# Ten more filler products on TensorE, and a new hand-written order for the opening of an attention and feed-forward kernel

## The chip, the cores and the metric

The kernel runs on one core of one Trainium2 chip. What counts is the device time of one execution in microseconds (us), as the median of several runs. Its engines are TensorE (PE in the profile, with its weight loads as PEld), VectorE (DVE), ScalarE (ACT), GpSimd (POOL) and SyncE (SP), whose queue issues the DMA transfers.

## What is computed

Attention over keys and values that are first averaged in groups of 8, then a gated feed-forward layer on its output, with weights given in 64-bit floating point. Cut to what matters:

```python
# q, k, v: (8 batches, 8 heads, 576, 64), float32; w_in (512, 2048), w_out (2048, 512), float64
k_p = k.reshape(B, H, Sp, 8, D).mean(axis=3)          # Sp = 72
v_p = v.reshape(B, H, Sp, 8, D).mean(axis=3)
scores = (q @ k_p^T) / sqrt(D)
attn = softmax(scores)                                # with max subtracted, sum + 1e-9
x = (attn @ v_p) as 4608 rows of 512
h = x @ w_in
out = (h * clip(h + 3, 0, 6) / 6) @ w_out
```

## The kernel before

The 4608 rows of x are worked in ten blocks (512, 256, 384, six of 512, 384). For each block TensorE makes h for one of 16 slices of d_ff (`Step.h`, L782: twelve products, three for each quarter c of d_model, since x and the weights are split into a high and a low part), ScalarE and VectorE gate it, and `Step.out` (L813) adds its products into the output. In the gaps of a block's steps the attention of the next block is made.

The first block has nothing ahead of it, so there is an opening: k and v of batch 0 are loaded and averaged, the scores of the first four tiles of 128 queries are made (half A, two tiles; half B, two tiles; two groups g of four heads each), the attention is transposed, multiplied with v, split into xhi and xlo, and meanwhile the first weights are turned from 64-bit words into float32 and split.

The steps of the opening that the texts name:

- `busy(n)` (L270): n products of the identity with itself into a PSUM tile `idle` that nobody reads. 13 stand first, 3 later.
- `prep_k` (L214 on VectorE, L222 on ScalarE): averages k. The first four (VectorE's 0 to 3) are batch 0; VectorE's 87, 93, 99 and 100 are the four of batch 1, which the opening doesn't need; 87 waits for the transfer kst that is SP's number 14.
- `Scores`: `product` (L412, TensorE), `top` (L416, VectorE, negative maximum), `exps` (L420, ScalarE), or for one tile of half A, called x11, `shift` (L427, VectorE), `exp` (L430, ScalarE) and `total` (L433, VectorE); then `invert` (L436, L437) and `divide` (L448, L454, on VectorE or GpSimd). x00, x10, x01, x11 are half A (the second digit is g); b[0] to b[3] are half B.
- `FirstValues.heads` (L290): sixteen products that average v; `transposes_of_half` (L507, L509), whose results VectorE or ScalarE copies (L510, L511). VectorE's number 54 is the copy for half B, g = 1: the last thing that the last two `av` of the block wait for.
- `av` (L583): attention times v, two products each; VectorE's `xlo` (L589) splits what comes out.
- `Prep` of weights: `scale` (L695) and `low` (L684) on ScalarE, `sign` (L689) and `join` (L700) on VectorE, `hi` (L723, ScalarE), `lo` (L728, VectorE). The h of slice f needs the `lo` of f.
- `pool_second` (L385, VectorE): averages v of batch 1.

Up to the fourth step of the first block the order of the instructions on every engine is not that of the program text. `put_in_order` takes the instructions of that window, numbers them for each engine in program order, and chains them in the order of the table `ORDER`. SP's entries are the order in which the loads are issued. An engine works strictly in its order, so an instruction that waits holds all that stand behind it.

Of the kernel before, what the change touches and what calls it, by code (L numbers as in the profile page):

```python
# [30 lines left out]

ORDER = {
    "PE": """
        0-12 17-18 13-16 19-45 50-53 56-57 46-49 54-55 60-63 58-59 64-68 78-79 69-71 80-85 88-89 72-74 86-87
        75-77 100-101 96-99 102-108 118-126 109-111 211-214 112-117 93-95 90-92 127-144 230-233 145-147 246-247
        148-156 166-171 157-159 163-165 266-267 160-162 193-195 184-189 172-180 190-192 196-198 181-183 218-223
        199-201 208-210 277-278 297-298 202-204 299 215-217 205-207 224-229 251-253 240-242 234-236 248-250
        243-245 237-239 254-259 279-281 260-262 268-270 263-265 274-276 315-316 282-287 306-308 288-296 334-336
        303-305 271-273 300-302 309-314 323-328 317-322 337-342 349-350 362-364 331-333 343-345 329-330 346-348
        354-356 365-367 357-359 368-376 385-387 360-361 380-381 351-353 382-384 388-390 377-379 391-393 419-421  # L40
        394-396 400-402 409-411 397-398 406-408 403-405 422-427 451-453 438-440 428-430 399 441-443 454-456
        431-433 416-418 457-462 444-446 412-415 479-481 466-468 434-437 476-478 469-472 447-450 463-465 482-493
        473-475 536-537 503-505 494-496 530-532 562-563 544-546 497-499 547-549 533-535 538-540 582-583 541-543
        500-502 512-514 509-511 550-555 515-517 506-508 556-558 518-523 576-578 559-561 564-569 579-581 524-526
        584-589 570-572 527-529 573-575
    """,
    "DVE": """
        3 2 1 0 4-8 87 11 15 9 12 17 16 10 18 13 19 14 20-21 23 22 24 26 34 28 40 64 29 25 61 32 30 33 62 36 35
        37 27 39 38 47 31 43-44 41 65 55 93 45 50 49 51 63 52-53 56 54 42 48 59-60 57-58 99 74 46 100 77 73 106
        76 75 79 81 78 82 111 80 107 121 86 108 83-84 112 67 110 85 113 90 88 109 89 68 94 114 91-92 115 131 96  # L50
        98 95 101 136 97 103 66 143 105 102 116 104 137 118 117 132 122 120 126 119 128 133 127 130 129 144 140
        123 138 147 139 142 141 72 149 145 70-71 146 124 69 152 125 135 148 151 150 154 156 134 159 153 157 155
        166 158 160-161 168 170 167 163 172 162 169 173 164-165 171 174-175 178-179 187 183 181 184-186 188 194
        176 189 182 177 190 199 191 180 200 192 201 193 195 197-198 202 196 203
    """,
    "Activation": """
        3 2 0-1 4-18 27 19 34 21 20 25 23 82 22 24 81 28-32 35-38 46 26 33 53 40-43 54 44 47-50 52 56 51 60 55
        39 59 69 89 61 57-58 45 88 74 96 95 71 67 70 75 68 97 104-107 98 72 76 79 73 80 77 108-111 86 78 83-84
        93 62 90 85 87 94 117-120 91 126-129 99 102 92 115 103 100 112 136 65 130 137 101 138-139 116 113 124
        121 114 125 122 140 123 143 66 63 131 64 132 134 144 135 153 133 145 141 147 142 150 148 146 154 151 149  # L60
        155 157 160 156 152 166 158 161 159 167 170-172 162-163 168 164 173 165 174 176 178 169 175 183 177
        180-181 179 187 186 184 188 185 194-197 189 202-205 198-199 182 200 208-211 190-191 201 206 192 207
        212-213 193
    """,
    "Pool": """
        0-1 12 2-3 18 4 7-8 10 5 9 6 14 13 16 15 17 11 19-20 24 21 23 22
    """,
    "SP": """
        2-3 1 0 4-5 8 6-7 14 9 11 10 22-24 21 20 13 12 15 18 16 19 25-26 28 31 17 27 32 34 33 29 41 30 44 51 35
        48 46 43 36 47 39 52 59 42 37-38 45 40 50 49 53-55 57-58 60 56  # L70
    """,
}

# [2 lines left out]
def attention_moe_kernel(  # L76
# [190 lines left out]
    def busy(n):  # L267

        for _ in range(n):
            nc.tensor.matmul(idle, ident, ident, start=True, stop=True)  # L270
# [609 lines left out]
    for s in x:  # L880
        s.product()
    values.rest()
    busy(3)
    values.heads(0)
    values.heads(1)
    for s in x:
# [211 lines left out]
```

## Time and profile before

| | |
|---|---|
| median of 3 runs | 924.62 us (923.67, 924.62, 924.62) |
| the profiled execution's own time | 923.03 us |
| span of the profiled execution, first to last instruction | 921.2 us |
| TensorE busy | 908.1 us (99%) |
| VectorE, ScalarE busy | 457.4 us (50%), 461.7 us (50%) |
| granted clock of TensorE, mean | 0.998 |

The profiled execution has 1.8 us outside of its span (923.03 less 921.2). The median of the three runs lies 1.6 us above it. Busy time of TensorE is modelled from starts and pipelined ends, so it says that TensorE has something in flight and not that it is at its peak.

### The profile page before, as it was taken

To read this page: it belongs to the slowest core of one execution; us is meant where nothing else is said; L and a number is where in the kernel's file an instruction comes from. 1 tells how busy PE (TensorE), PEld (TensorE's weight loads), DVE (VectorE), ACT (ScalarE), POOL (GpSimd) and SP (SyncE) were. 2 spreads that over 40 slices of the span, in tenths; PEclk is the share of its full clock that TensorE was granted. 3 is DMA by queue.
4 is the path that set the end of the run, shared out by engine and by line. 5 is a ranking of instruction groups with operands and counts; after the bars stand their busy time and mean duration, and the time that the engine had idled before them with its cause. 6 is when DMAs were issued, how large, how long until landed. Compare 5 with 4: busy or idle time off the path is not lost.

```text
span 921.2 us, 12671 instructions
## 1 busy us (share of the span) xinstructions
PE 908.1 (99%) x4548; PEld 776.8 (84%) x4548; DVE 457.4 (50%) x916; ACT 461.7 (50%) x1340; POOL 82.0 (9%) x167
## 2 busy tenths in 40 slices
PE   7899999999999999999999999999999999999998
PEld 7688889999888888888888888888888888888997
DVE  6999855475356333824356326633356234332322
ACT  6898665465355434633456335633545344333322
POOL 4100001021000100101011101110101001100000
PEclk9999999999999999999999999999999999999999
DMA  9960203050031002300042004100210010000100
GB/s 313 393 242 1 92 12 121 1 166 19 0 115 58 24 1 80 104 12 6 1 145 57 12 1 134 61 12 1 92 42 23 1 41 18 0 1 3 45 1 35
DMA packets 41935, 57.19 MB, mean 62 GB/s; under 512 B 7568, under 2 KB 23696, under 8 KB 41872
## 3 DMA queue, kind: packets, MB, share of 16 engines
q1 hardware_dynamic: 41728, 56.37, 19.0%
q8 instruction: 36, 0.59, 0.3%
q14 instruction: 27, 0.22, 0.1%
q10 hardware_dynamic: 144, 0.00, 0.0%
HBM read 46.93 MB, written 9.44 MB: 61 GB/s over the span
## 4 chain that ended last, share of the span: by engine, by line
PE 96%; DVE 2%; DMA 1%; SPq 0%; ACT 0%; issue 0%; DVEq 0%
PE pso L813 43%; PE psh L782 43%; PE psa L583 4%; PE psa L412 4%; PE psa L518 2%; DMA kst<-k_l 1%; PE psa L520 0%; DVE u L689 0%; ACT stage L420 0%; DVE u L700 0%; SPq L257 0%; DVE stage L448 0%; SPq L259 0%; DVE a L510 0%; SPq L262 0%
## 5 line engine op out<-in xcount | busy, mean ns | idle before, releaser
L782 PE MATMUL psh<-xhi,w 128*128 128x512 f32 (+2 forms) x1288 | 402.3, 372 | 0.0
L813 PE MATMUL pso<-w,ghi 128*128 128x512 f32 (+1 forms) x1184 | 367.0, 391 | 0.0
L782 PEld LDWEIGHTS psh<-xhi,w 128*128 128x128 f32 x1288 | 238.0, 188 | 36.1 <-issue 0.4
L813 PEld LDWEIGHTS pso<-w,ghi 128*128 128x128 f32 x1184 | 214.1, 188 | 36.0
L782 PE MATMUL psh<-xlo,w 128*128 128x512 f32 (+2 forms) x644 | 237.5, 369 | 0.0
L794 DVE SCALAR_TENSOR_TENSOR g<-g,psh 128x512 f32<-128x512 f32 (+2 forms) x161 | 101.4, 630 | 271.6 <-ACT g L790 270.4
L813 PE MATMUL pso<-w,glo 128*128 128x512 f32 (+1 forms) x592 | 225.9, 386 | 0.0
L790 ACT ACTIVATE g<-psh,small 128x512 f32<-128x512 f32 (+2 forms) x161 | 103.7, 644 | 209.7 <-PE psh L782 193.3
L782 PEld LDWEIGHTS psh<-xlo,w 128*128 128x128 f32 x644 | 121.3, 188 | 18.2
L802 DVE TENSOR_TENSOR glo<-g,ghi 128x512 fp32r<-128x512 f32 (+2 forms) x161 | 102.7, 638 | 62.1 <-ACT ghi L798 60.2
L813 PEld LDWEIGHTS pso<-w,glo 128*128 128x128 f32 x592 | 111.1, 188 | 21.7
L798 ACT CAST ghi<-g 128x512 fp32r<-128x512 f32 (+2 forms) x161 | 92.9, 577 | 70.6 <-DVE g L794 67.9
L420 ACT ACTIVATE e<-psa,mx 128x72 f32<-128x72 f32 x256 | 78.5, 322 | 50.8 <-DVE mx L416 50.1
L448 POOL TENSOR_TENSOR a<-e,sm 128x256 f32<-128x256 f32 x60 | 41.2, 687 | 517.2 <-PE pso L813 180.3
L420 ACT ACTIVATION_READ_ACCUMULATOR e<-psa,mx 128x1 f32 x256 | 52.8, 206 | 0.0
L416 DVE TENSOR_REDUCE mx<-psa 128x4 f32<-128x288 f32 x72 | 32.3, 454 | 29.2 <-PE psa L412 28.8
L412 PEld LDWEIGHTS psa<-kbd,qt 128*128 128x128 f32 x288 | 43.1, 189 | 4.2
L412 PE MATMUL psa<-kbd,qt 128*128 128x144 f32 x288 | 45.5, 285 | 0.0
L585 ACT COPY x<-psa 128x192 f32<-128x192 f32 (+7 forms) x60 | 23.0, 387 | 32.6 <-PE psa L583 32.4
L332 DVE TENSOR_REDUCE vsum<-vst 128x64 f32<-128x512 f32 (+1 forms) x36 | 37.8, 1068 | 2.3 <-DMA vst<-v_l 1.5
L436 DVE TENSOR_SCALAR sm<-sm 128x4 f32<-128x4 f32 x72 | 12.4, 176 | 48.7 <-ACT e L420 45.7
L529 ACT CAST ahi<-psa 128x256 fp32r<-128x256 f32 (+1 forms) x70 | 24.6, 353 | 18.8 <-PE psa L518 9.8
(93 smaller groups left out, 628.9 us busy)
## 6 DMA issues: line engine op xcount, KB each, us to landing
out<-o SPq DMA_DIRECT2D x35, 256.0 KB, 2.3
raw<-w_in_l SPq DMA_DIRECT2D x16, 512.0 KB, 8.4
raw<-w_out_l SPq DMA_DIRECT2D x16, 512.0 KB, 9.1
kst<-k_l SPq DMA_DIRECT2D x28, 288.0 KB, 3.2
qt<-q_l SPq DMA_DIRECT2D x28, 256.0 KB, 3.2
vst<-v_l SPq DMA_DIRECT2D x24, 256.0 KB, 3.0
vst<-vr_l SPq DMA_DIRECT2D x36, 64.0 KB, 1.9
stage<-k_l SPq DMA_DIRECT2D x4, 288.0 KB, 3.6
```

The costliest lines, as they stand in the source:

```text
L332: nc.vector.tensor_reduce(out=vs[:n, p], in_=st[:n, : POOL * D].rearrange("p (o d) -> p d o", o=POOL), axis=AX.X, op=ALU.add)
L412: nc.tensor.matmul(to, qt[:, p, :], kbds[b % 2][:, p, :], start=r == 0, stop=r == last)
L416: nc.vector.tensor_reduce(out=self.mx, in_=self.ps, axis=AX.X, op=ALU.max, negate=True)
L420: nc.scalar.activation(self.e[:, h], self.ps[:, h], AF.Exp, bias=self.mx[:, h : h + 1], accum_out=self.sm[:, h : h + 1])
L448: engine.tensor_tensor(out=self.a[:, : 4 * D].rearrange("p (h s) -> p h s", h=4), in0=e[:, :, :D], in1=sm[:, :, None].broadcast_to([P, 4, D]),
L583: nc.tensor.matmul(ps, l, r, start=n == 0, stop=n == len(mms) - 1)
L782: nc.tensor.matmul(self.ps, l[f][:, c, :], r[:, c, :], start=c == 0 and i == 0, stop=c == NCC - 1 and i == 2)
L790: nc.scalar.activation(self.g, self.ps, AF.Relu, bias=half, scale=1.0 / (6.0 * WSCALE))
L794: nc.vector.scalar_tensor_tensor(out=g, in0=g, scalar=1.0, in1=self.ps, op0=ALU.min, op1=ALU.mult)
L798: nc.scalar.copy(self.ghi, self.g)
L802: nc.vector.tensor_tensor(out=self.glo, in0=self.g, in1=self.ghi.bitcast(F32), op=ALU.subtract)
L813: nc.tensor.matmul(pos, l, r[:, cols], start=f == 0 and i == 0, stop=f == NF - 1 and i == 2)
```

## The change

`busy(3)` between the scores' products and `values.heads` becomes `busy(13)`: ten more products that nobody reads. In program order they are TensorE's numbers 24 to 33, so that every later number of TensorE's list is 10 higher than before (`heads` was 24 to 39 and is 34 to 49). And `ORDER`, the whole table, is another one. The first lines of each engine, before and after; the other lines of the lists of TensorE, VectorE and ScalarE are replaced too:

```diff
 "PE"
-0-12 17-18 13-16 19-45 50-53 56-57 46-49 54-55 60-63 58-59 64-68 78-79 69-71 80-85 88-89 72-74 86-87
-75-77 100-101 96-99 102-108 118-126 109-111 211-214 112-117 93-95 90-92 127-144 230-233 145-147 246-247
+0-12 21 13-14 22 15-18 23 19-20 24 34-49 62-63 25 50-55 26 66-67 64-65 68-69 27-28 56-59 74-75 60-61
+70-71 88-89 72-73 29-30 76-81 31 90-93 32 82-87 33 94-95 98-99 96-97 106-121 128-130 122-124 131-136
 "DVE"
-3 2 1 0 4-8 87 11 15 9 12 17 16 10 18 13 19 14 20-21 23 22 24 26 34 28 40 64 29 25 61 32 30 33 62 36 35
-37 27 39 38 47 31 43-44 41 65 55 93 45 50 49 51 63 52-53 56 54 42 48 59-60 57-58 99 74 46 100 77 73 106
+0 3 1-2 4-6 87 7-9 11 15 12 10 13 17 14 18 26 23 22 24 19 16 32 20 33 28-29 93 21 25 64 55 65 27 35 34
+43 40 36 30 37 31 38-39 61 99 50 41 44 51 47 45 52-53 62 49 56 54 48 100 42 59 57 46 60 58 74 63 73
 "Activation"
-3 2 0-1 4-18 27 19 34 21 20 25 23 82 22 24 81 28-32 35-38 46 26 33 53 40-43 54 44 47-50 52 56 51 60 55
+0-15 17 16 19 18 82 20 28-31 21 25 81 53 24 54 26 22-23 27 34-38 32 88 33 40-43 89 47-50 39 46 44 56 52
 "Pool"
-0-1 12 2-3 18 4 7-8 10 5 9 6 14 13 16 15 17 11 19-20 24 21 23 22
+0-1 12 2-3 18 7 4 8 11 5-6 13 9-10 17 14-16 19-22 24 23
 "SP"
-2-3 1 0 4-5 8 6-7 14 9 11 10 22-24 21 20 13 12 15 18 16 19 25-26 28 31 17 27 32 34 33 29 41 30 44 51 35
+3 0-2 4-5 8 7 14 6 9-10 13 12 15 23-24 22 11 16 20-21 19 17-18 25-26 28-29 32 34 30-31 33 27 48 41 44 51
@@ between the scores of half A and values.heads(0) @@
-    busy(3)
+    busy(13)
```

In words, for what the texts speak of. On TensorE: of the thirteen fillers that now stand at the second `busy`, four lie between the products of half A's scores, one after them, and the rest singly or in pairs between the later groups; the last is ahead of 84 and 85 (before's numbers; 94 and 95 after), the transposes of half B's last 32 columns, g = 0. The product of b[0] goes ahead of half A's transposes. What stands ahead of the last two `av` of the block is the same work as before, besides fillers. On VectorE: 87 goes ahead of `top` and `shift` of x11 (7 and 8); 99 goes ahead of 54, and 63 (a `pool_second` piece) behind it. On ScalarE: 17, the `scale` of the first weights, goes ahead of 16, the `exp` of x11. On SP: kst (14) goes ahead of vr (6), the second half of q (10) ahead of the second part of the first weights (11).

## Rows read from the trace of the kernel before

**Rows 1.** The page, busy time of each engine over the span.
```profile
PE 908.1 (99%) x4548; PEld 776.8 (84%) x4548; DVE 457.4 (50%) x916; ACT 461.7 (50%) x1340; POOL 82.0 (9%) x167
```

**Rows 2.** The chain that ended last: start us, us, what.
```profile
5.59 7.24 DMA kst<-k_l
...
33.41 0.61 DVE a L510
...
34.07 3.50 PE psa L583 x8
```

**Rows 3.** Windows: stretch, length, PE, PEld, DVE, ACT, POOL busy (instructions), clock, DMA share, GB/s.
```profile
10.00:15.00 5.00, 3.35 (x30) 3.16 (x29) 3.15 (x15) 4.31 (x24) 3.18 (x5) 1.00 1.04 380
...
200.00:921.00 721.00, 717.50 (x3501) 610.19 (x3499) 310.71 (x634) 318.75 (x949) 57.36 (x114) 1.00 0.13 38
```

**Rows 4.** The same columns, microsecond by microsecond around 34 us.
```profile
34.00:35.00 1.00, 0.93 (x3) 0.82 (x4) 1.00 (x4) 1.00 (x2) 0.00 (x0) 0.69 1.07 342
35.00:36.00 1.00, 1.00 (x4) 0.82 (x3) 1.00 (x2) 0.96 (x3) 0.00 (x0) 0.50 1.03 393
36.00:37.00 1.00, 1.00 (x4) 0.74 (x3) 1.00 (x2) 0.56 (x2) 0.00 (x0) 0.50 1.04 414
37.00:38.00 1.00, 1.00 (x6) 0.91 (x5) 0.28 (x1) 0.39 (x2) 0.00 (x0) 0.60 1.03 410
```

**Rows 5.** Windows, PE alone: stretch, length, busy (instructions), clock, DMA share, GB/s.
```profile
10.40:34.07 23.67, 16.65 (x110) 1.00 1.05 373
```

**Rows 6.** Windows, DVE alone, same columns: ahead of and behind the copy of half B.
```profile
12.85:34.01 21.16, 20.71 (x53) 1.00 1.05 372
...
34.01:49.64 15.63, 14.32 (x21) 0.89 1.04 397
```

**Rows 7.** Timeline of PE: start us, us, instruction, count, idle before it and releaser.
```profile
9.65 0.83 PE L270 MATMUL idle<-ident 128*128 128x128 f32 x6
12.13 3.84 PE L290 MATMUL psa<-stage,ident 128*128 128x128 f32 x32 [1.65 <-DMA stage<-v_l]
...
17.61 1.22 PE L412 MATMUL psa<-kbd,stage 128*128 128x144 f32 x8 [0.77 <-DMA stage<-q_l]
...
32.48 0.60 PE L507 MATMUL psa<-ident,stage 128*128 128x128 f32 x4
34.07 0.94 PE L583 MATMUL psa<-a,v 128*128 128x256 f32 x2 [0.98 <-DVE a L510]
...
50.13 0.63 PE L782 MATMUL psh<-xhi,w 128*128 128x512 f32 x2
```

**Rows 8.** Timeline of DVE, same columns.
```profile
8.87 1.68 DVE L416 TENSOR_REDUCE mx<-psa 128x4 f32<-128x288 f32 x4 [1.54 <-PE psa L412]
10.58 0.46 DVE L427 TENSOR_TENSOR stage<-psa,mx 128x288 f32<-128x288 f32 x1
12.85 0.75 DVE L214 TENSOR_REDUCE ksum<-kst 128x72 f32<-128x576 f32 x1 [1.81 <-DMA kst<-k_l]
14.36 0.41 DVE L448 TENSOR_TENSOR stage<-stage,sm 128x256 f32<-128x256 f32 x1
...
30.96 0.39 DVE L385 TENSOR_TENSOR v<-v 128x256 f32<-128x256 f32 x1
...
33.33 0.68 DVE L510 COPY a<-psa 128x512 f32<-128x512 f32 x1
...
48.42 1.23 DVE L728 TENSOR_TENSOR w<-u,w 128x1024 fp32r<-128x1024 f32 x1
```

**Rows 9.** Timeline of ACT, same columns.
```profile
12.94 0.51 ACT L430 ACTIVATE stage<-stage 128x288 f32<-128x288 f32 x1
14.13 0.68 ACT L695 ACTIVATE raw<-raw 128x512 f32<-128x512 f32 x1 [0.69 <-DMA raw<-w_in_l]
```

**Rows 10.** Windows, all engines: what the DMA engines moved (last column, GB/s).
```profile
4.00:12.80 8.80, 7.15 (x49) 6.96 (x48) 5.02 (x9) 4.72 (x27) 1.71 (x2) 1.00 1.05 335
...
14.10:17.60 3.50, 2.74 (x25) 2.51 (x24) 3.50 (x11) 3.35 (x7) 3.38 (x6) 1.00 1.08 304
```

More of the change, by code (lines that the diff above doesn't have):

```diff
@@ L33 @@
     "PE": """
-        0-12 17-18 13-16 19-45 50-53 56-57 46-49 54-55 60-63 58-59 64-68 78-79 69-71 80-85 88-89 72-74 86-87
-        75-77 100-101 96-99 102-108 118-126 109-111 211-214 112-117 93-95 90-92 127-144 230-233 145-147 246-247
-        148-156 166-171 157-159 163-165 266-267 160-162 193-195 184-189 172-180 190-192 196-198 181-183 218-223
-        199-201 208-210 277-278 297-298 202-204 299 215-217 205-207 224-229 251-253 240-242 234-236 248-250
-        243-245 237-239 254-259 279-281 260-262 268-270 263-265 274-276 315-316 282-287 306-308 288-296 334-336
@@ L39 @@
[L39 to L43, printed above, removed]
@@ L44 @@
-        500-502 512-514 509-511 550-555 515-517 506-508 556-558 518-523 576-578 559-561 564-569 579-581 524-526
-        584-589 570-572 527-529 573-575
+        0-12 21 13-14 22 15-18 23 19-20 24 34-49 62-63 25 50-55 26 66-67 64-65 68-69 27-28 56-59 74-75 60-61
+        70-71 88-89 72-73 29-30 76-81 31 90-93 32 82-87 33 94-95 98-99 96-97 106-121 128-130 122-124 131-136
+        125-127 100-102 137-139 221-224 240-243 103-105 140-148 152-154 149-151 155-157 256-257 158-160 179-181
+        176-178 161-163 173-175 170-172 164-169 182-184 203-205 200-202 185-193 197-199 194-196 225-227 231-233
@@ new lines @@
+        206-211 218-220 212-217 276-277 234-239 261-263 228-230 258-260 244-249 253-255 264-272 250-252 281-283
+        278-280 287-291 273-275 292-294 307-309 284-286 295-297 313-315 310-312 304-306 298-303 319-321 316-318
+        325-326 344-346 322-324 333-335 327-332 336-338 359-360 341-343 364-366 372-374 347-352 361-363 375-377
+        353-355 378-380 390-391 381-386 339-340 356-358 367-369 395-400 370-371 392-394 387-389 401-406 410-412
+        429-431 407-408 413-415 432-437 409 438-440 416-418 448-450 441-443 419-421 426-428 444-447 451-453
@@ L46 @@
+        422-425 476-478 454-460 464-466 479-482 467-472 546-547 473-475 461-463 492-494 483-485 495-497 572-573
+        498-503 489-491 486-488 510-512 504-509 592-593 540-542 516-518 543-545 522-524 554-556 548-553 557-562
+        513-515 566-568 563-565 519-521 525-527 569-571 574-576 528-530 586-588 577-579 589-591 594-596 531-533
+        597-599 534-539 583-585 580-582
     """,
     "DVE": """
-        3 2 1 0 4-8 87 11 15 9 12 17 16 10 18 13 19 14 20-21 23 22 24 26 34 28 40 64 29 25 61 32 30 33 62 36 35
@@ L49 @@
-        37 27 39 38 47 31 43-44 41 65 55 93 45 50 49 51 63 52-53 56 54 42 48 59-60 57-58 99 74 46 100 77 73 106
[L50 to L53, printed above, removed]
@@ L54 @@
-        176 189 182 177 190 199 191 180 200 192 201 193 195 197-198 202 196 203
+        0 3 1-2 4-6 87 7-9 11 15 12 10 13 17 14 18 26 23 22 24 19 16 32 20 33 28-29 93 21 25 64 55 65 27 35 34
+        43 40 36 30 37 31 38-39 61 99 50 41 44 51 47 45 52-53 62 49 56 54 48 100 42 59 57 46 60 58 74 63 73
+        76-77 79 106 75 81 78 82 80 111 84 83 66 86 88 85 121 68 90 89 67 112 92 91 94 96 95 98 101 97 103 113
+        107 102 108 105 110 109 116 131 104 118 115 117 114 120 126 136 128 119 143 138 122 130 127 71 70 72 69
@@ L55 @@
+        137 129 123 140 142 139 149 144 125 141 147 145 132 152 148 151 124 154 146 156 133 150 159 134 157 153
+        155 166 158 161 160 135 168 163 167 164-165 162 169 172-173 170 175 171 187 174 178 194 179 176 195 188
+        196 189 186 183 177 181 184-185 182 180 199 190 200 191-193 197-198 201-203
     """,
     "Activation": """
-        3 2 0-1 4-18 27 19 34 21 20 25 23 82 22 24 81 28-32 35-38 46 26 33 53 40-43 54 44 47-50 52 56 51 60 55
-        39 59 69 89 61 57-58 45 88 74 96 95 71 67 70 75 68 97 104-107 98 72 76 79 73 80 77 108-111 86 78 83-84
@@ L59 @@
[L59 to L63, printed above, removed]
+        0-15 17 16 19 18 82 20 28-31 21 25 81 53 24 54 26 22-23 27 34-38 32 88 33 40-43 89 47-50 39 46 44 56 52
@@ new lines @@
+        60 96 51 55 95 59 45 57 69 98 58 70 97 67 71 68 62 74-76 72 104-107 73 79 77 61 80 83 78 108-111 66 86
+        84 87 65 85 90 93 91 94 99 102 92 103 100 115 112 101 116 113 63 117-120 64 121 114 126-129 124 131 136
+        125 122 137-138 134 130 123 135 153 132 144 139 143 140 133 147 150 141 145 142 148 146 160 155 154 162
+        157 149 151 166 161 152 156 158-159 163 167 171 164-165 168 170 172 169 175 173 178-179 174 180 183
+        194-197 181 176-177 189 202-205 188 187 186 184 182 185 198 208-211 199-201 206 190 207 191 212 192 213
@@ L64 @@
+        193
     """,
     "Pool": """
-        0-1 12 2-3 18 4 7-8 10 5 9 6 14 13 16 15 17 11 19-20 24 21 23 22
+        0-1 12 2-3 18 7 4 8 11 5-6 13 9-10 17 14-16 19-22 24 23
     """,
     "SP": """
-        2-3 1 0 4-5 8 6-7 14 9 11 10 22-24 21 20 13 12 15 18 16 19 25-26 28 31 17 27 32 34 33 29 41 30 44 51 35
-        48 46 43 36 47 39 52 59 42 37-38 45 40 50 49 53-55 57-58 60 56
+        3 0-2 4-5 8 7 14 6 9-10 13 12 15 23-24 22 11 16 20-21 19 17-18 25-26 28-29 32 34 30-31 33 27 48 41 44 51
@@ L71 @@
+        47 43 35 52 36 40 39 37-38 45-46 42 50 49 59 53-54 56 58 55 57 60
     """,
```

## The prediction

> **What bounds the kernel now.** I read the page first: TensorE is busy for 99% of the span [rows 1], so the end moves only with time in which TensorE has nothing to do or runs slowly. The windows say where that is: hardly any after 200 us, some in the opening [rows 3]. Between 10.40 and 34.07 us TensorE is busy for 16.65 of 23.67 us, so it waits for 7.02 us [rows 5]; from 34.07 on it never stops. The chain of waits confirms it: before 34.07 us the chain runs over a transfer and over VectorE, and at 34.07 it passes to TensorE, from VectorE's copy for half B (number 54), and stays there [rows 2]. The moment at which that copy ends, 34.01 us, decides when the unbroken stretch begins [rows 7, 8].
>
> The second loss is the clock. In the windows around 34 us the granted clock falls to half (1.2 of 2.4 GHz) just after TensorE takes up its work, and is full again before 38 us [rows 4]. What TensorE did before: it ended its transposes at about 33.1 us and stood until 34.07, after a stretch of short pieces of work [rows 5, 7]. The missing shares are 0.31 + 0.50 + 0.50 + 0.40 of a microsecond, together 1.71 us of full-speed work, and TensorE had work for all of it [rows 4].
>
> What sets the copy's time? VectorE's windows: from 12.85 us, when kst lands and 87 starts, to 34.01 us it is busy for 20.71 of 21.16 us [rows 6]. Ahead of that it stood for 1.81 us, waiting for kst, with nothing behind it that it could have done sooner than its order allows [rows 8]. So the opening before is bound by VectorE, from the landing of kst to 54.
>
> **The fillers.** Three fillers show six records; the last five starts are (0.83 - 0.27) us apart in total, 0.11 us each, with some 0.27 us for the last one alone, so a filler takes 0.22 us [rows 7]. Ten take 2.2 us. They are free if they fall into waits, of which there are 7.02 us [rows 5]; the last one stands ahead of two transposes of half B, after which TensorE still waits for VectorE twice. I take nothing; without that cover they cost up to 2.2 us.
>
> **VectorE's order.** Up to and with 54 its list is the same set of instructions, except that 99 comes in (as long as 87, 0.75 us) and 63 goes out (0.39 us) [rows 8]. More important is 87: it now stands ahead of x11's `top` (one of four in 1.68 us: 0.42) and `shift` (0.46). Before, these two ran while VectorE would have waited for kst anyhow; now they wait behind 87 and are done after the landing [rows 8]. From 87 to the end of 54 VectorE therefore has 20.71 + 0.42 + 0.46 + 0.75 - 0.39 = 21.95 us of work.
>
> It starts when kst lands. SP issues it one place earlier, ahead of vr with its 128 KB; at the 335 GB/s of that stretch this is 0.38 us [rows 10], so 12.47 us. Without any wait 54 ends at 34.42 us.
>
> Two waits come in. First, x11's `exp` on ScalarE stands behind `scale` of the first weights, which starts when these land, at 14.13 us, and takes 0.6 net; `exp` takes 0.5, so it ends at about 15.2 [rows 9]. VectorE reaches `total` after 87, 7, 8, five small ones at some 0.08 and a divide of 0.41: 12.47 + 0.75 + 0.42 + 0.46 + 0.40 + 0.41 = 14.9. Wait: 0.3 to 0.4, I take 0.35. Second, `top` of b[0] needs b[0]'s product, which before waited until 17.61 us for the second half of q [rows 7]. q now goes right behind the first weights: 14.13 us plus 512 KB at 304 GB/s, 1.7 us [rows 10], is 15.8, and I take 16.0, since its pieces are small. Product and latency add 0.7: 16.7. VectorE is there at 15.2 + 0.35 (`total`) + 0.5 (divide) + 0.05 = 16.1. Wait: 0.6. Were q as late as before, 17.61, it would be 2.2. So 54 ends at 34.42 + 0.35 + 0.60 = 35.4, between 34.4 (no wait) and 37.0 (0.35 and 2.2). GpSimd's vr lands later too, by the 288 KB of kst (0.9 us), but half A's transposes then find b[0]'s product ahead of them, which hides it; other waits behind ScalarE I count as nothing, since I step through about even with VectorE there.
>
> TensorE so takes up the last two `av` at 35.45 instead of 34.07: a loss of 1.4 us (0.4 to 3.0).
>
> **The clock.** With fillers between the groups the clock should stay full, and 1.71 us come back. No filler stands in the last wait, which is now longer: all work ahead of the copy is done by about 33.1 us as before, so TensorE stands for 2.3 us where it stood for 0.98 [rows 7]. Below, this is the rival.
>
> **Does the stream stay unbroken?** Before, VectorE had `lo` of slice 3 ready at 48.42 + 1.23 = 49.65 us and TensorE used it first at 50.13 + 0.23: some 0.7 us ahead [rows 7, 8]. After the change VectorE's work from 54 to there is 14.32 - 0.75 + 0.39 = 13.96 us [rows 6, 8], ending at 49.4 without waits. TensorE's need, with the full clock, comes (50.36 - 34.07) - 1.71 = 14.6 us after 35.45, at 50.0. So it holds, with 0.6 us to spare; VectorE waited 1.31 us in that stretch before [rows 6], and if it does so again TensorE loses up to 0.7. I take nothing, and keep 0.7 for the range.
>
> Sum: +1.4 - 1.7 = -0.3 us. The profiled execution's span goes from 921.2 to 920.9, its time from 923.03 to 922.7; the median of 924.62, which lies 1.6 above it, to 924.3.
>
> **The rivals.**
>
> 1. *The clock falls all the same.* The fillers stand early, and the wait ahead of the copy grows from 0.98 to 2.3 us. For it: half speed came before after a shorter wait. Against: the work before that wait is denser (fillers, and groups gathered). It is decided by whether half speed is granted between 33 and 37 us. Price: the -1.71 is gone, +1.4, and with VectorE's waits +0.7: 926.0 to 926.7, slower. This is also the case that the change doesn't do what it says.
>
> 2. *The timed runs of before never had the fall.* One profile shows it, and I can't see the others; their median is even longer. Then nothing comes back, and +1.4 stays: 926.0. What speaks against it is only the one trace in hand [rows 4]. The Trainium skill bears on this: "TensorE: Matmul & The Clock Gate", Part 1, says that the switching isn't tied to the kernel's start, so that its moment differs between runs of one kernel; no row here shows that, since there is one trace.
>
> 3. *VectorE doesn't lose its place.* If kst landed by 10.2 us, when `top` of x10 is done [rows 8], 87 would cost no wait, and 54 would end 2.3 us earlier than I say, at 33.1; with the clock full: 924.62 - 0.9 - 1.7 = 922.0, faster. Against it: kst landed at 12.83 [rows 2], and one place in the queue is 0.38 us.
>
> **Chances.** Forecast 0.60; its own range is -1.3 (54 at 34.4, full clock) to +2.0 (54 at 37.0 and 0.7 for `lo`), so 923.3 to 926.6. Rival 1 0.18, rival 2 0.14, rival 3 0.08. The bound of 0.2%, about what a measurement can tell, is 1.85 us. Faster than that is rival 3 and a little more: 0.10. Slower than that is half of rival 1, a third of rival 2 (each with the later VectorE) and the top of the forecast's range: 0.22. Same: 0.68. For 8 in 10 I take 922.6 to 926.9: at the low end the forecast's end and 0.7 for rival 3, at the high end rival 1 with its waits.
>
> **What would show it.** Right: VectorE's first batch-1 reduction at about 12.5 us with two instructions of x11 behind it; the copy for half B ending near 35.4; no half clock; an unbroken TensorE from there; ScalarE's `scale` ahead of `exp` at 14.1. Wrong: half clock in 33 to 38 us (rival 1); other profiles of before without it (rival 2); the copy before 34 us (rival 3); waits of TensorE for `lo` after 40 us; q landing near 17.6.

## The result, and the profile after

The changed kernel takes 927.68 us (median of 6 runs, 926.51 to 928.86), against 923.35 us for the kernel before, timed beside it (6 runs, 921.42 to 924.62): a ratio of 1.0048, 95% interval 1.0031 to 1.0064. It is slower by 4.3 us, beyond the range of 922.6 to 926.9. The profiled execution of it took 928.31 us with a span of 926.2 us, 5.0 us more than the span before. One later run of the kernel before took 1521.48 us at a mean granted clock of 0.557 and is left out of every figure.

One thing that stands ahead of the prediction has to be put right. The table's window ends at the fourth step of the *second* block (`j == 1 and u == 3`), at about 143 us, so the table orders the whole first block too. And what the table does not name is put in order when the program is recorded, starting from where the table ends: a comparison of the two traces, engine by engine, shows other orders up to about 225 us, and the same order from there on.

The opening first. Windows of the kernel after answer to [rows 3 to 6]; the columns are stretch, length, busy of PE, PEld, DVE, ACT, POOL (instructions), clock, DMA share, GB/s:

```profile
10.40:36.89 26.49, 20.08 (x134) 16.57 (x132) 23.33 (x56) 21.99 (x84) 8.97 (x16) 1.00 1.05 360
12.93:36.84 23.91, 18.16 (x118) 14.84 (x116) 23.00 (x55) 19.41 (x67) 8.97 (x16) 1.00 1.05 365
36.84:49.64 12.80, 12.75 (x69) 11.17 (x70) 12.72 (x19) 11.69 (x25) 0.00 (x0) 1.00 1.05 387
```

No half clock, as forecast. VectorE is still the engine that sets the end of the opening: busy for 23.00 of 23.91 us from the landing of kst to the copy for half B. But that stretch was to be 22.9 us long (21.95 of work and 0.95 of waits), and kst was to land at 12.47. VectorE's timeline after answers to [rows 8]:

```profile
12.93 0.75 DVE L215 TENSOR_REDUCE ksum<-kst 128x72 f32<-128x576 f32 x1 [2.25 <-DMA kst<-k_l]
13.60 0.45 DVE L417 TENSOR_REDUCE mx<-psa 128x4 f32<-128x288 f32 x1
14.08 0.46 DVE L428 TENSOR_TENSOR stage<-psa,mx 128x288 f32<-128x288 f32 x1
14.45 0.78 DVE L437 TENSOR_SCALAR sm<-sm 128x4 f32<-128x4 f32 x3
...
15.41 1.07 DVE L449 TENSOR_TENSOR stage<-stage,sm 128x256 f32<-128x256 f32 x1
...
17.32 0.44 DVE L417 TENSOR_REDUCE mx<-psa 128x4 f32<-128x288 f32 x1
...
24.00 0.69 DVE L386 TENSOR_TENSOR stage<-stage 96x512 f32<-96x512 f32 x1 [0.88 <-DMA stage<-vr_l]
...
36.16 0.68 DVE L511 COPY a<-psa 128x512 f32<-128x512 f32 x1
```

The order is the one described: 87, then x11's `top` and `shift`, both now behind the landing. The copy ends at 36.84 us, where 35.4 was forecast. The two waits for `exp` and for b[0]'s product did not come (no bracket at 14 to 18 us). Instead three small instructions at 14.45 took 0.78 us and a divide at 15.41 took 1.07, where the same divide took 0.41 [rows 8], and a transfer of vr is waited for at 24.00. GpSimd's timeline shows what ran beside them: its two large additions of vr, which in the kernel before ran from 11.01 to 13.06 us, since vr was then issued ahead of kst.

```profile
13.80 2.06 POOL L302 TENSOR_TENSOR stage<-stage 32x512 f32<-32x512 f32 x2 [10.05 <-DMA stage<-vr_l]
```

ScalarE and TensorE, against [rows 7, 9]. ScalarE's `scale` is ahead of `exp`, b[0]'s product starts at 16.41 us (17.61 before), and TensorE takes up the last two `av` at 36.89 instead of 34.07:

```profile
14.80 0.69 ACT L696 ACTIVATE raw<-raw 128x512 f32<-128x512 f32 x1 [1.54 <-DMA raw<-w_in_l]
15.38 0.44 ACT L431 ACTIVATE stage<-stage 128x288 f32<-128x288 f32 x1
```
```profile
16.41 0.73 PE L413 MATMUL psa<-kbd,stage 128*128 128x144 f32 x4 [0.85 <-DMA stage<-q_l]
...
35.71 0.38 PE L510 MATMUL psa<-ident,stage 128*96 128x128 f32 x2
36.89 0.70 PE L584 MATMUL psa<-a,v 128*128 128x256 f32 x2 [0.79 <-DVE a L511]
```

Now what the prediction did not look for. Two windows of the stretch that was to stay unbroken, before and then after (columns as above):

```profile
140.00:150.00 10.00, 10.00 (x67) 9.10 (x67) 4.46 (x12) 4.55 (x16) 2.71 (x6) 1.00 0.61 178
200.00:210.00 10.00, 10.00 (x56) 9.17 (x55) 8.79 (x20) 7.85 (x28) 1.50 (x3) 1.00 0.33 94
```
```profile
140.00:150.00 10.00, 9.23 (x55) 7.83 (x54) 3.44 (x10) 5.72 (x18) 2.09 (x5) 1.00 0.57 174
200.00:210.00 10.00, 8.74 (x45) 7.14 (x44) 8.65 (x18) 7.27 (x29) 1.47 (x4) 1.00 0.52 136
```

TensorE was busy throughout both before, and stands in both after. At 140 us the timelines of TensorE, of its weight loads and of ScalarE say why:

```profile
140.01 0.39 PE L814 MATMUL pso<-w,glo 128*128 128x512 f32 x1
141.17 0.73 PE L814 MATMUL pso<-w,ghi 128*128 128x512 f32 x2 [0.77 <-ACT o L820]
```
```profile
141.17 0.30 PEld L814 LDWEIGHTS pso<-w,ghi 128*128 128x128 f32 x2 [1.19 <-ACT o L820]
```
```profile
140.21 0.40 ACT L799 CAST ghi<-g 128x256 fp32r<-128x256 f32 x1 [1.96 <-PE pso L814]
140.52 0.59 ACT L820 ACTIVATE o<-pso 128x512 f32<-128x512 f32 x1
```

TensorE can go on when ScalarE has emptied a PSUM bank (`o`). That copy stands in ScalarE's order behind a `ghi` which itself waits, for 1.96 us, for TensorE. The weight loads stand for 1.19 us there; this is the wait that the experiments look for.

At 200 us VectorE holds the stream up. VectorE after:

```profile
196.60 0.52 DVE L795 SCALAR_TENSOR_TENSOR g<-g,psh 128x384 f32<-128x384 f32 x1
198.56 2.05 DVE L333 TENSOR_REDUCE vsum<-vst 128x64 f32<-128x512 f32 x2 [1.43 <-DMA vst<-v_l]
200.53 0.55 DVE L803 TENSOR_TENSOR glo<-g,ghi 128x384 fp32r<-128x384 f32 x1
...
203.86 0.55 DVE L795 SCALAR_TENSOR_TENSOR g<-g,psh 128x384 f32<-128x384 f32 x1
```

The averaging of the next v waits for its transfer and stands ahead of `glo`, which TensorE needs. Before, `glo` stood ahead of the same pair, which waited for 0.31 us:

```profile
195.06 0.55 DVE L802 TENSOR_TENSOR glo<-g,ghi 128x384 fp32r<-128x384 f32 x1
...
196.01 2.05 DVE L332 TENSOR_REDUCE vsum<-vst 128x64 f32<-128x512 f32 x2 [0.31 <-DMA vst<-v_l]
```

TensorE after waits several times between 201 and 204.5 us, the last two of them:

```profile
203.37 0.76 PE L413 MATMUL psa<-kbd,qt 128*128 128x144 f32 x4 [0.93 <-ACT e L421]
204.47 0.45 PE L783 MATMUL psh<-xhi,w 128*128 128x384 f32 x1 [0.34 <-DVE g L795]
```

How far the profiled execution of after lies behind that of before can be counted by the work that TensorE has done (the products of each trace added up at their usual lengths, fillers left out). The lag is 2.8 us at 34 us and 1.2 at 38 us, because the execution before has lost 1.7 us to its half clock in between. It is 1.0 at 100 us, 2.4 from 143 us, and 4.55 from 230 us to the last product; the rest of the 5.0 lies behind that. So the stretch around 140 us costs 1.3 us and the one around 200 us 2.2.

### The profile page after: what moved, and what is told of

It reads as the page before. It is cut to its first block, busy times and chain, and to the rows that moved or that the text cites. A ratio compares the mean times of both kernels' runs of the same rounds, so it can differ in the third digit from the quotient of the medians.

```text
span 926.2 us, 12708 instructions
## 1 busy us (share of the span) xinstructions
PE 911.2 (98%) x4568; PEld 778.1 (84%) x4568; DVE 457.5 (49%) x916; ACT 461.0 (50%) x1340; POOL 79.2 (9%) x167
## 4 chain that ended last, share of the span: by engine, by line
PE 94%; DMA 3%; DVE 1%; SPq 1%; ACT 0%; issue 0%; DVEq 0%
PE pso L814 42%; PE psh L783 42%; PE psa L584 4%; PE psa L413 4%; PE psa L519 1%; DMA raw<-w_out_l 1%; DMA raw<-w_in_l 1%; DMA vst<-v_l 1%; PE psa L521 0%; DVE vsum L333 0%; DVE v L386 0%; SPq L258 0%; DVE a L511 0%; SPq L260 0%; ACT stage L421 0%
```

## The experiments

Every kernel here fixes the order of all instructions, to the end of the program, so that the rest can't be put in another order by an edit of the opening:

```diff
+        window[1:] = [len(traced)]      # the table now names every instruction
```

"Old" and "new" are the orders before and after. The kernel before was timed again beside them, four times: medians 922.76 (27 runs), 923.06 (27), 922.93 (32) and 923.29 (17). Numbers 1 to 4 belong to the first, 5 to 8 to the second, 9 to 12 to the third, 13 and 14 to the fourth. "Full clock" below means a mean granted clock of 0.999 or 1.0: in the profiles of numbers 2 and 14, which have 0.999, the clock is full as long as TensorE works from 5 us on and falls only in the last 2 us, behind its last product.

**1. Old order everywhere, fixed.** What the fixing itself does, and whether the half clock is always there.

> The kernel before, with the order of every engine written out to the end, the same order that it had: its time is that of before. Its runs list the granted clock of each execution. Theory (the half clock is a matter of chance): some executions have a mean clock of 0.998 and some 1.0, and those with the full clock are up to 1.7 us shorter. Rival (the half clock belongs to this order): every execution has 0.998.

922.95 us, ratio 1.0011 (1.0001 to 1.0022): near nothing. The runs of the kernel before beside it have a mean granted clock of 1.0 in 11 of 27; these average 922.05 us, the 12 with 0.998 average 923.38. Over all four timings 41 of 103 runs have 1.0 and 61 have 0.998 or less, and the difference between 1.0 and 0.998 is 1.3 to 2.2 us. So a half clock like that of [rows 4] is an event of some executions, and rival 2 was right for four in ten. A run lists the mean alone, not the place. The profiles show that the place differs as well: the clock is half from about 34 to 40.6 us in number 1's, and from about 13.3 to 16.7 us in number 9's, whose 922.37 us is the fastest of its eleven runs.

**2 and 3. New opening with the old rest, and old opening with the new rest.** The table's part (to about 143 us) from one order, what stands behind it from the other.

```diff
 # 2: new_opening_old_rest                     # 3: old_opening_new_rest
-"PE" <old table>  <old rest>                  -"PE" <old table>  <old rest>
+"PE" <new table, with fillers>  <old rest>    +"PE" <old table>  <new rest>
```

> The changed kernel's opening (table and fillers), and behind it, to the end of the program, the order that the kernel before had. Theory (the rest of the program was put in another order, and that costs some 3.5 us at 141 us and at 201 to 204 us): span about 922.3, 1 us above before, and no wait of TensorE at these two places. Rival (the opening hands on its lateness, and the waits come whatever the order of the rest): span 925 to 926, as the changed kernel.

> The opening of the kernel before with three fillers, and behind it the order that the rest of the changed kernel had. Theory (the order of the rest costs some 3.5 us): span about 924.7, with TensorE's waits near 140 us and 200 us. Rival (the lateness of the opening makes them): span 921 to 922.

Measured: 925.82 (1.0031, 1.0019 to 1.0044) and 925.29 (1.0028, 1.0018 to 1.0039). Both halves of the change cost. In 2 the copy ends at 35.80, the wait of 1.19 us stands at 140.08, and TensorE doesn't stop near 200 us:

```profile
140.08 0.30 PEld L900 LDWEIGHTS pso<-w,ghi 128*128 128x128 f32 x2 [1.19 <-ACT o L906]
```
```profile
200.00:210.00 10.00, 10.00 (x54) 9.05 (x53) 9.09 (x22) 7.03 (x25) 1.04 (x2) 1.00 0.41 112
```

In 3 it is the reverse; windows of 3:

```profile
140.00:150.00 10.00, 10.00 (x67) 9.06 (x66) 4.39 (x12) 4.68 (x17) 2.70 (x6) 1.00 0.59 171
200.00:210.00 10.00, 8.73 (x48) 7.75 (x47) 8.66 (x20) 7.67 (x32) 1.34 (x4) 1.00 0.43 112
```

**4. New opening without the ten fillers** (`busy(3)`, the numbers of TensorE's table shifted back; the rest old).

```diff
-    busy(13)
+    busy(3)
-"PE" 0-12 21 13-14 22 15-18 23 19-20 24 34-49 62-63 25 50-55 26 66-67 ...
+"PE" 0-12 21 13-14 22 15-18 23 19-20 24-39 52-53 40-45 56-57 ...
```

> As the new opening with the old rest, without the ten fillers. Theory (they fall into waits and cost nothing): the same time within 0.3 us where the clock is full, and the half clock in more of the executions, which are then 1 to 1.7 us longer. Rival (fillers delay work that somebody waits for): up to 2.2 us shorter.

925.08 (1.0026, 1.0015 to 1.0037), 0.7 us below number 2 with overlapping intervals. The full-clock runs, six of each, average 924.95 without the fillers and 924.92 with them, and from the landing of kst to the copy the profiles take 22.9 and 22.8 us: no price of the fillers is seen. One of 7 runs has a mean clock of 0.998 or less, with the fillers 4 of 10: no sign that the fillers keep the clock.

**5. New order up to the block's first `av`, then old.**

```diff
-"DVE" 0 3 1-2 4-6 87 7-9 ... 49 56 54 48 100 42 59 57 ...
+"DVE" 0 3 1-2 4-6 87 7-9 ... 49 56 54 63 42 48 59-60 57-58 ... (old order from here)
```

> The new table and its fillers only up to the last two av of the first block (the end of VectorE's late copy); from there the order of before on every engine, to the end. Theory (the new opening costs only the later copy, 1.5 to 2 us, and the other 1.2 us come from a wait at 140 us that the new table's later lines make): median 924.5, no wait of TensorE near 140 us. Rival (all 3 us are the opening): median 925.8 as with the whole new table.

925.55 (1.0022, 1.0012 to 1.0032), a miss. The wait at 140 us is gone. The weight loads stand for 0.42 us at 45.48, for VectorE's gate, for 0.76 at 96.41 and for 0.53 at 156.64; the last two have their like in the old order (0.38 at 94.50 in the kernel before, 0.79 at 156.55 in number 1), so they are not shown to come from this one. What else keeps this kernel slow is open. This execution had the half clock; windows around it, microsecond by microsecond:

```profile
36.00:37.00 1.00, 1.00 (x4) 0.73 (x4) 1.00 (x2) 1.00 (x2) 0.00 (x0) 0.50 1.14 348
37.00:38.00 1.00, 1.00 (x5) 0.81 (x3) 1.00 (x2) 0.57 (x3) 0.00 (x0) 0.50 1.04 365
38.00:39.00 1.00, 1.00 (x6) 0.91 (x5) 0.95 (x3) 0.53 (x2) 0.00 (x0) 0.50 1.03 401
```

VectorE is busy throughout. The four runs with a clock of 1.0 average 925.78 and the five with 0.998 average 925.74, but one of the four took 927.47 us, so the runs don't tell whether a full clock gave something back here.

**6. New opening, 87 behind `top` and `shift` of x11 again.**

```diff
-"DVE" 0 3 1-2 4-6 87 7-9 11 15 ...
+"DVE" 0 3 1-2 4-8 87 9 11 15 ...
```

> The new table with the old rest, but VectorE's 87, the reduction that waits for kst, again behind top and shift of x11 (7 and 8). Theory (87 holds these two behind the landing): the copy for half B ends 0.8 us earlier, near 35.0, and the median falls from 925.8 by 0.8 to 925.0. Rival (the waits for the loads and for ScalarE set that time): no change.

924.82 (1.0021, 1.0011 to 1.0031). The median is 1.0 us below number 2's, as the theory had it, but not for its reason: the full-clock runs average 924.81 and 924.92, and the copy ends 22.74 us after the start of 87, against 22.82 in number 2. The 0.9 us did not come back. Three small instructions, which now start together with GpSimd's first addition of vr and not near its end, took it (1.40 us; 0.49 in number 2):

```profile
12.84 0.75 DVE L301 TENSOR_REDUCE ksum<-kst 128x72 f32<-128x576 f32 x1 [1.29 <-DMA kst<-k_l]
13.51 1.40 DVE L523 TENSOR_SCALAR sm<-sm 128x4 f32<-128x4 f32 x3
```

**7. New opening with the old order of the loads** (SP's list alone is the old one).

```diff
-"SP" 3 0-2 4-5 8 7 14 6 9-10 13 12 15 ...
+"SP" 2-3 1 0 4-5 8 6-7 14 9 11 10 22-24 ...
```

> The new table with the old rest, but SP's list of loads is that of before. Theory (the new order of loads makes vr, the second part of the first weights and the rest pieces of batch 1 late, and these hold ScalarE and VectorE): the copy ends 0.5 to 1.5 us earlier, the median falls below 925.3. Rival (the loads don't matter, or q, which comes later in the old list, holds b[0] back): the copy is as late or later, up to 37 us.

942.16 (1.0207, 1.0188 to 1.0225). The copy ends at 41.40, and TensorE waits for 9.6 us at 82.38, for a `ghi` of ScalarE that stands behind the `scale` of weights that land late. The loads and the engines' lists are one plan, and the run says nothing of kst by itself.

**8. Old table, ten fillers in the two last waits of the opening** (six ahead of the transposes 100 and 101, four behind 99, in before's numbers).

> The kernel before with ten fillers more: six ahead of the transposes 100 and 101 and four behind 99, in the two last waits of TensorE before the late copy; nothing else is changed. Theory (fillers in these waits hold the clock): mean clock 1.0 in nearly every execution, median 922.0, as before's executions at the full clock. Rival 1 (fillers don't hold it): as many executions at 0.998 and below as before, median 922.8. Rival 2 (they delay the copies): the copy ends later, median above 923.

922.35 (0.9995, 0.9986 to 1.0004). Four of 11 runs have 0.998, none less; before, beside it, 16 of 27 have 0.998 or less. The direction is the expected one, but the time isn't resolved from the kernel before.

**9. Old table, 87 early alone; 10. old table, vr late alone.** The two moves that I then held to be behind the later copy, each by itself.

```diff
 # 9
-"DVE" 3 2 1 0 4-8 87 11 15 ...
+"DVE" 3 2 1 0 4-6 87 7-8 11 15 ...
 # 10
-"SP" 2-3 1 0 4-5 8 6-7 14 9 11 ...
+"SP" 2-3 1 0 4-5 8 7 14 6 9 11 ...
```

> The order of before with one thing moved: VectorE's 87 ahead of top and shift of x11 (7 and 8), as in the changed table. Theory (87 holds these two behind the landing of kst, and nothing hides that): the late copy ends 0.8 us later after the landing of kst than before, 22.0 us instead of 21.2, and the median rises by 0.8. Rival (x11's sum waits for ScalarE anyhow): 21.2 us, no change.

> The order of before with one thing moved: the load of vr (6) behind that of kst (14), as in the changed table. Theory (vr then lands 2 us later, GpSimd adds its pieces while VectorE works, and VectorE's instructions last longer beside it): VectorE's small instructions and its divide after the landing of kst take up to 1.5 us more, the copy ends 0.5 to 1 us later. Rival (GpSimd's work is hidden): kst lands 0.4 us earlier, and the copy too.

Number 9: the copy ends 22.13 us after the start of 87. In the kernel before it was 21.16 [rows 6], and 21.1 to 21.4 in the profiles of numbers 1, 3 and 13, which share its opening: +0.7 to +1.0, where the prediction has 0.42 + 0.46. The time is 923.4 (1.0004, 0.9993 to 1.0014); full-clock runs 923.12 against 922.33 before. Number 10: 924.93 (1.0015, 1.0006 to 1.0025). VectorE and then GpSimd in 10:

```profile
12.03 0.75 DVE L300 TENSOR_REDUCE ksum<-kst 128x72 f32<-128x576 f32 x1 [1.14 <-DMA kst<-k_l]
12.70 1.55 DVE L522 TENSOR_SCALAR sm<-sm 128x4 f32<-128x4 f32 x3
...
15.32 1.32 DVE L540 TENSOR_TENSOR stage<-stage,sm 128x96 f32<-128x96 f32 x1
16.56 1.13 DVE L534 TENSOR_TENSOR stage<-stage,sm 128x256 f32<-128x256 f32 x1
```
```profile
12.90 2.06 POOL L387 TENSOR_TENSOR stage<-stage 32x512 f32<-32x512 f32 x2 [9.14 <-DMA stage<-vr_l]
```

kst lands 0.8 us earlier, as one would wish, and the copy yet ends 1.5 us later. The three small instructions take 1.55 us, beside the first addition; the two divides take 1.32 and 1.13, beside GpSimd's last, small addition and its own divides. Before, the three took 0.50, and the two divides 0.58 and 0.56, also beside divides of GpSimd:

```profile
13.52 0.50 DVE L436 TENSOR_SCALAR sm<-sm 128x4 f32<-128x4 f32 x3
...
14.78 0.58 DVE L454 TENSOR_TENSOR stage<-stage,sm 128x96 f32<-128x96 f32 x1
15.28 0.56 DVE L448 TENSOR_TENSOR stage<-stage,sm 128x256 f32<-128x256 f32 x1
```

**11 and 12. New opening with vr ahead of kst; the same with 87 back.** If that collision were the whole of the excess, the opening would be mended.

```diff
 # 11 and 12
-"SP" 3 0-2 4-5 8 7 14 6 9-10 ...
+"SP" 3 0-2 4-5 8 6-7 14 9-10 ...
 # 12 also
-"DVE" 0 3 1-2 4-6 87 7-9 11 15 ...
+"DVE" 0 3 1-2 4-8 87 9 11 15 ...
```

> The new table with the old rest, but with the load of vr (6) again ahead of v's second half and kst. Theory (GpSimd's additions of vr beside VectorE's work lengthen it): VectorE's work from the landing of kst to the copy falls from 22.8 to about 22.0 us, the copy ends near 35.2, median 925.2. Rival (the lateness is in the order of the instructions): 22.8 us, and the copy 0.4 us later with kst.

> The same with 87 behind 7 and 8 as well. Theory (both the collision and 87 cost, and moving 87 alone was eaten by the collision): 21.2 us from the landing of kst to the copy, as before, the copy near 34.3, median 924.3. Rival (ScalarE's scale ahead of exp holds x11): 22 us or more, no better than with vr alone.

926.14 (1.0027, 1.0015 to 1.004) and 925.9 (1.0025, 1.0014 to 1.0037): both missed. The collision with the two large additions is gone (three small ones 0.30 us, the divide 0.42; a single small one at 16.29, beside the last addition, takes 1.18), but the second half of q lands later, and in 11 VectorE waits for b[0]'s product:

```profile
14.87 0.30 DVE L523 TENSOR_SCALAR sm<-sm 128x4 f32<-128x4 f32 x3
...
18.60 0.46 DVE L503 TENSOR_REDUCE mx<-psa 128x4 f32<-128x288 f32 x1 [1.12 <-PE psa L499]
```

This is the wait that the prediction put at 0.6 to 2.2 us. After the change it is absent: VectorE, late already, reaches that `top` at 17.32 us, when the product (16.41 + 0.73) is done.

**13 and 14. Where the wait at 140 us comes from.** 13: old order up to the first `av`, then the new table's lines, old rest. 14: new table up to about 115 us, then the old order. The lists of 14 leave the new table at these places:

```diff
 "Activation"
-... 178-179 174 180 183 194-197 181 176-177 189 202-205 ... <old rest>
+... 178-179 174 176 183 177 180-181 187 186 184 188 185 194-197 ... <old rest>
 "PE"
-... 454-460 464-466 479-482 467-472 546-547 ... <old rest>
+... 454-456 461-472 489-491 486-488 479-482 457-460 ... <old rest>
```

> Old order up to the block's first attention times v (about 30 us), the new table's lines from there to its end at 143 us, the old order of the rest pinned behind. If the new table's later lines make the wait at 140 us by themselves, it stands at about 138 us here with 1.2 us, the copy for half B ends near 34 to 35, and the time is 1.2 us above the kernel before (923.4 to 924.5). If the later opening is what makes it, there is no such wait and the time is that of the kernel before (922 to 923).

> The new table up to about 115 us, then the old order to the end. If the wait at 140 us comes from the new table's last lines, it is gone, and the time is 1.2 us under that of the whole new opening with the old rest (925.8), 924.6; the copy for half B stays near 35.8. If it comes from the order ahead of 115 us, it stays, and the time is 925.8.

13 took 937.46 us (1.015, 1.0131 to 1.0169): as in number 7, lists and loads don't match, and TensorE stands for some 10 us at 77.8 behind late weights. But the wait at stake is there, with ScalarE's `o` behind `ghi`, though the start is the old one. In 14 it is gone. The weight load of 13, and the window of 14:

```profile
152.77 0.30 PEld L899 LDWEIGHTS pso<-w,ghi 128*128 128x128 f32 x2 [1.19 <-ACT o L905]
```

```profile
140.00:150.00 10.00, 10.00 (x67) 9.06 (x66) 3.85 (x11) 4.56 (x16) 2.70 (x6) 1.00 0.52 155
```

14 took 923.78 us (1.0006, 0.9994 to 1.0018), no measurable difference to the kernel before by all runs, although its copy ends at 36.10 (11 of before's 17 runs beside it have 0.998; the full-clock runs alone do differ, see below). So the new table's last lines make the wait, whichever opening stands ahead of them.

## Why the prediction was wrong

The full-clock runs alone leave the half clocks of chance out. Among them number 14, which keeps the new opening, is 923.50 - 921.95 = 1.55 us above the kernel before beside it (9 and 6 runs). Number 2 is 924.92 - 922.14 = 2.8 above (6 and 12 runs), so the table's last lines add 1.2. The new rest adds 924.17 - 922.14 = 2.0 (number 3, 2 runs; its six runs with 0.998, against before's with 0.998, give 2.2). Together that is 4.8 to 5.0; the changed kernel's four runs at full clock average 927.15, 5.0 above 922.14. The groups are small and single runs in them spread over 1 to 3 us, so the parts are good to some tenths; the two profiles give 1.3 and 2.2 for the last two. The medians differ by less than 5.0, by 4.3; the six runs of before list no clock, but where they are listed half clocks are in more of its runs.

- **The step that failed: "Does the stream stay unbroken?"** The prediction tested it up to 50 us, for `lo` of slice 3, where it held, and took the stream behind as given, at no cost. It broke at 140 us, by the table's own last lines (1.2 us, numbers 2 and 14), and near 200 us, by the order of what the table doesn't name (2.0 to 2.2 us, number 3). With 3.2 to 3.4 of 5.0 us it is the larger part of the loss.
- **The clock's -1.71** was mis-sized. The half clock was a feature of one trace: about six runs of before in ten have a mean clock below 1.0. Removing it everywhere would give, by an estimate from these runs, 0.6 x 1.3 to 2.2, so 0.8 to 1.3 us. Part of that came: the changed kernel and numbers 2, 4, 5, 6, 11, 12 and 14, which share its opening in the main, have 0.998 or less in 31 of 79 runs, the kernel before in 61 of 103. The Trainium skill, "TensorE: Matmul & The Clock Gate", Part 1, which the prediction cites beside rival 2, says that the moment of switching isn't tied to the kernel's start. The profiles agree: with the same order of TensorE's work the fall comes at 34 us (before, number 1) or at 13 us (number 9). The fillers are not shown to be behind what came (number 4).
- **VectorE's order, +1.4**, had the right mechanism, and its size came near by luck. Number 14 puts the opening at 1.55 us. From the landing of kst to the copy the profiles of numbers 2, 4, 5 and 14 take 22.8 to 23.0 us, where 22.9 was forecast, but not by the forecast's terms: in number 2 VectorE is busy for 22.78 of 22.82 us, so the 0.95 of waits isn't in it, and longer instructions stand in their place. 87 ahead of two instructions of x11 costs 0.7 to 1.0 us to the copy (number 9; 0.88 forecast). Not seen: GpSimd's additions of vr move beside VectorE's small instructions and lengthen them (number 10). The prediction noted that vr lands later, and asked only who waits for the result, not what the additions slow. kst landed at 12.93, not at 12.47; over the profiles with this order of loads it lands between 12.40 and 13.13, with the old order between 12.65 and 13.26, so the one place in the queue is lost in that. Both foreseen waits stayed away: q came earlier, as forecast, and VectorE was late. In the changed kernel 0.88 us more is the wait for vr at 24.00, which number 2 doesn't have. The copy's end varies from profile to profile of new openings (35.2 to 36.8 us), so the share of each cause isn't settled to better than some tenths.
- **The fillers at nothing** held: number 4 shows no price of theirs.
- **The start of the sum**, 924.62 us from three runs, was 1.3 us above the median of the six. The range lies too high by that, and the result is above it even so.
- **Rival 1** (half clock all the same) didn't come in the profile, and its reason didn't either: TensorE stood for 0.79 us ahead of the last two `av`, not for 2.3, since its last transposes come later as well. **Rival 3** (kst early) did not happen.

Not settled: whether a later copy costs all of its delay under the old table. With the copy at 35.0, 35.5 and 35.15 us (34.01 before), numbers 9, 10 and 8 lose 0.8, 1.15 and 0.2 us among full-clock runs (5, 2 and 7 of them), but the full-clock runs of the kernel before alone lie between 920.9 and 923.6. In the profile of number 9 nothing is made up: TensorE is 1.0 us behind the execution before at 34 us, and once that one's half clock is taken off it stays so to the end.

## What to carry to other kernels

Before costing an edit in a hand-written order, find the last instruction that the order names, and ask what arranges the rest: an edit in the opening can move work hundreds of microseconds later, and "unchanged from there on" has to be read from the two orders. Two engines' lists and the order of the loads are one plan, of which no piece can be put back by itself (+19 us in number 7). A clock event in one trace may be chance until several executions show it.

## What the hardware showed unexpectedly

- Some VectorE instructions grow while GpSimd adds, others don't. Three on 128x4 elements took 0.50 us after GpSimd's two large additions had ended (13.06 us in the kernel before) and 0.30 in numbers 9 and 11, but 0.49, 0.78, 1.40 and 1.55 us beside them (numbers 2, after, 6 and 10). The trace's single records show what sets the length: the one that starts while the first addition runs ends 0.03 us after it in all four (14.86 after 14.83 us, 15.10 after 15.07, 14.76 after 14.73, 14.19 after 14.15). A divide of 128x256 took 0.41 and, beside the second addition, 1.07 us. `top` and `shift`, which read PSUM, took 0.45 and 0.46 us beside the same additions, as [rows 8] have them without (0.42, 0.46). GpSimd's own additions took 2.05 and 2.06 us in both cases.
- The same program, run again, has a mean granted clock of 1.0 in 41 of 103 executions and less in the others. The length of TensorE's last stand doesn't decide it. In the profile of before the fall followed a stand of 0.98 us [rows 4, 7]; after the change it stood for 0.75, 0.96 and 0.79 us (at 32.28, 35.25 and 36.89) and kept the full clock. But number 9 also stood for 0.98 us, at 35.06, and kept it there, and number 5 stood for 0.79, at 35.29, and lost it.
